# Backward weights loaded by transposing DMAs instead of TensorE transposes and a trip through DRAM

## The chip, the core and the metric

The kernel runs on one core of a Trainium2 chip. The metric is the device time of one execution in microseconds (us); three runs of the kernel before gave 1393.33, 1394.78 and 1395.50, median 1394.78. A core has five engines that run their own instruction streams: TensorE (PE; weight loads are shown as PEld), VectorE (DVE), ScalarE (ACT), GpSimd (POOL) and SyncE (SP). In this kernel SP issues nearly all DMAs; ScalarE issues those of the last stage.

## The reference, cut to what matters

Four residual layers, A, B, A, B, on a sequence of 2048 tokens of width 512 in bf16, with the same weights in both A layers and in both B layers. The outputs are the forward result and the gradients of the input and of five weight matrices.

```python
def _A_ref(x, wqkv, wo):            # wqkv (512, 1536), wo (512, 512), 32 heads of 16
    qkv = ...                        # x @ wqkv, split in q, k, v
    phi = lambda t: jnp.where(t > 0, t + 1, jnp.exp(t)) + 1e-6
    pq, pk = phi(q), phi(k)
    kv = jnp.einsum("bhsd,bhse->bhde", pk, v)
    z = jnp.einsum("bhsd->bhd", pk)
    ...
    o = num / den
    return o... @ wo
def _B_ref(x, w_gate, w_up, w_down): # (512, 1376), (512, 1376), (1376, 512)
    h = _sigmoid(x @ w_gate) * (x @ w_up)
    return h @ w_down
x = x + _A_ref(_layernorm(x), A_wqkv, A_wo)
x = x + _B_ref(_layernorm(x), B_w_gate, B_w_up, B_w_down)
x = x + _A_ref(_layernorm(x), A_wqkv, A_wo)
x = x + _B_ref(_layernorm(x), B_w_gate, B_w_up, B_w_down)
# and jax.vjp of all this against grad_out
```

Forward, a weight is used as it lies in DRAM. Backward, the gradient with respect to a layer's input needs each weight transposed: wdT, wuT, wgT for a B layer, woT and wqkvT for an A layer.

## The kernel before, in words

The sequence is cut into 16 tiles of 128 tokens (index `st`). The residual stream stays in SBUF as 16 tiles `x`. The stages follow each other as the program text has them; a scheduler then fixes the order of each engine's instructions ahead of the run, and may move instructions of a later stage into gaps of an earlier one. Each engine runs its list in order. A DMA waits in its queue for its data, for its destination to be free, and for the eighth DMA before it (eight semaphores are used in turn).

Start: `load_stream` (L95-109) loads x in four batches, with wqkv in between; x is cast to f32 on VectorE and ScalarE, `layernorm_tile` makes the normalised tile `hstage` (L310, ScalarE), and TensorE transposes it (`ln_tp`, L318).

Forward A layer, `a_fwd`. First half, for each tile: 12 matmuls with wqkv (`mm_ps`, L468), the exponentials, pq and pk, and four transposes of pq (`tp`, L318 by a helper). Then the small products kv and z. Second half, for each tile: `num_ps`, `den_ps`, the division (`ostage`), four transposes (`tp`), four matmuls with wo into `y_ps` (L542), a copy by ScalarE (L545) and the addition to x by GpSimd (L546).

Into the first half of both A layers, from tile 4 on, the caller puts a list of extra work, `extra`: the groups of `wT_groups` (L346-402), 26 of them in layer 0 and 24 in layer 2. A group transposes up to four blocks of 128x128 of a weight that lies in SBUF for the forward pass (TensorE, L372 for wg, wu, wqkv and wo; L396 for wd), into one PSUM tile `wt_ps`, which has one buffer; VectorE (L353) or ScalarE (L355) in turn copies it to a stage in SBUF, and SP stores the stage to DRAM (L377, L383, L400). The extra PSUM pool takes one of eight banks, so `mm_ps` has five buffers instead of six and `y_ps` one instead of two in these layers.

Forward B layer, `b_fwd`: gate and up products, sigmoid, transposes of the hidden tile, product with wd.

Backward: `b_bwd_p1(3)`, `a_bwd_p1(2)`, `b_bwd_p2(3)`, `b_bwd_p1(1)`, `a_bwd_p2(2)`, `a_bwd_p1(0)`, `b_bwd_p2(1)`, `a_bwd_p2(0)`. The p1 stages go through the tiles and make input gradients; the p2 stages make weight gradients with long sums over all tokens, and the scheduler moves their matmuls into the p1 stages where it can.

Each p1 stage starts with its weights. `load_b_weights` (L213-221) loads wdT, wuT and wgT, `load_a_weights` (L223-227) woT and wqkvT, all from the DRAM copies that the forward stages stored, on SP's queue. The pool for them has three places with one buffer each: w_a (wuT or wqkvT), w_b (wgT or woT) and w_c (wdT). So a load waits until the last use of what lay there. The first load of wdT waits for the end of the forward pass, as its SBUF was in use until then. In `b_bwd_p1`, `dhh_ps` (L760) uses wdT and `dh_ps` (L742) uses wuT and then wgT; in `a_bwd_p1`, `do_ps` (L958) uses woT and `dh_ps` (L1038) wqkvT. The loads `ssd_ld` (L751), `o_ld` and `pq_ld` (L696) and `p_set` (L811) go through the same queue.

Of the kernel before, what the change touches and what calls it, by code (L numbers as in the profile page):

```python
# [8 lines left out]
BF16 = mybir.dt.bfloat16  # L9
# [8 lines left out]
D = 512  # L18
# [32 lines left out]
def kernel(  # L51
# [70 lines left out]
    for l in range(4):  # L122
# [11 lines left out]
    k.wT = dict(  # L134
        wqkvT=dram.tile([3 * D, D], BF16, name="wqkvT_d"),
        woT=dram.tile([D, D], BF16, name="woT_d"),
        wgT=dram.tile([F, D], BF16, name="wgT_d"),
        wuT=dram.tile([F, D], BF16, name="wuT_d"),
        wdT=dram.tile([D, F], BF16, name="wdT_d"),
    )  # L140
# [11 lines left out]
    with tc.tile_pool(name="wfwd", bufs=1) as wfwd:  # L152
# [17 lines left out]
        with ExitStack() as lctx:  # L170
# [7 lines left out]
            if phases != "fwd":  # L178
                wtg = wT_groups(k)
                half = 26  # L180
                with tc.tile_pool(name="wt_stage", bufs=2) as wt_stage:
                    a_fwd(k, 0, lns[0], nxt=lns[1],
                          extra=lambda ps_pool: [g(wt_stage, ps_pool) for g in wtg[:half]])
                b_fwd(k, 1, lns[1], nxt=lns[2])
                with tc.tile_pool(name="wt_stage2", bufs=2) as wt_stage:
                    a_fwd(k, 2, lns[2], nxt=lns[3],
                          extra=lambda ps_pool: [g(wt_stage, ps_pool) for g in wtg[half:]])
            else:
                a_fwd(k, 0, lns[0], nxt=lns[1])
                b_fwd(k, 1, lns[1], nxt=lns[2])  # L190
                a_fwd(k, 2, lns[2], nxt=lns[3])
# [17 lines left out]
    with ExitStack() as bctx:  # L209
# [3 lines left out]
        def load_b_weights():  # L213
            k.wdT = wb.tile([P, NDC, F], BF16, name="wdT", tag="w_c")
            nc.sync.dma_start(out=k.wdT[:], in_=k.wT["wdT"].rearrange("(c p) f -> p c f", p=P))
# [130 lines left out]
def wT_groups(k):  # L346
    nc = k.nc
    groups = []
    cnt = [0]

    def evac(dst, src):
        if cnt[0] % 2 == 0:
            nc.vector.tensor_copy(dst, src)  # L353
        else:
            nc.scalar.copy(dst, src)  # L355
        cnt[0] += 1

    for w_sb, wT_d, C in ((k.wg, k.wT["wgT"], F), (k.wu, k.wT["wuT"], F),
                          (k.wqkv, k.wT["wqkvT"], 3 * D), (k.wo, k.wT["woT"], D)):
        ncc = (C + P - 1) // P  # L360
        for cc0 in range(0, ncc, 4):
            ccs = list(range(cc0, min(cc0 + 4, ncc)))
            holder = {}
            for j, cc in enumerate(ccs):
                def g(stage, ps_pool, w_sb=w_sb, wT_d=wT_d, C=C, cc0=cc0, ccs=ccs, j=j, cc=cc, holder=holder):
                    if j == 0:
                        holder["t"] = stage.tile([P, 4, D], BF16, name="wt_st")
                    st_t = holder["t"]
                    r = min(P, C - cc * P)
                    ps = ps_pool.tile([P, NDC, P], BF16, name="wt_ps")  # L370
                    for rc in range(NDC):
                        nc.tensor.transpose(ps[0:r, rc, :], w_sb[:, rc, cc * P:cc * P + r], k.ident[:])  # L372
                    evac(st_t[0:r, j, :], ps[0:r, :, :].rearrange("p a b -> p (a b)"))
                    if j == len(ccs) - 1:
                        nfull = len([c_ for c_ in ccs if min(P, C - c_ * P) == P])
                        if nfull > 0:
                            nc.sync.dma_start(  # L377
                                out=wT_d[cc0 * P:(cc0 + nfull) * P, :].rearrange("(n p) d -> p n d", p=P),
                                in_=st_t[:, 0:nfull, :])
                        if nfull < len(ccs):  # L380
                            c_ = ccs[nfull]
                            r_ = C - c_ * P
                            nc.sync.dma_start(out=wT_d[c_ * P:c_ * P + r_, :], in_=st_t[0:r_, nfull, :])  # L383
                groups.append(g)
    for cc in range(NDC):
        holder = {}
        for fs in range(3):
# [722 lines left out]
```

## Time and profile before

| what | value |
|---|---|
| median of three runs | 1394.78 us (1393.33 to 1395.50) |
| profiled execution, span from the first to the last instruction | 1393.1 us; the page has no other time of it |
| DMA traffic | 269.77 MB, mean 194 GB/s |
| transposes of `wt_ps` (L372, L396) | 196, each 218 ns long, between 34.0 and 290.6 us |
| copies of `wt_ps` (L353, L355) | 25 of about 0.42 us on VectorE, 25 of about 0.58 us on ScalarE |
| issue of wdT, wqkvT, woT, and issue to landing | 482.8 and 633.4 us, 6.6 to 6.9; 640.3 and 1025.8, 7.4 to 7.6; 642.7 and 1028.2, 6.5 to 6.7 |
| wuT and wgT main parts | 484.7 and 788.6 us; 488.9 and 701.7 us; 7.1 to 10.1 us to landing |
| first use of wdT, wuT, wgT, woT, wqkvT | 489.5, 498.0, 501.6, 650.2, 707.0 us |

The profile comes from one profiled execution. "Busy" of TensorE counts each matmul's whole way through the array, and matmuls overlap, so the distance from one start to the next tells more of the cost than a duration does. An arrow `<-` after an idle time names what ended the wait. "SPq" is SP's queue; the time beside a DMA there is its issue, not its transfer.

### The profile page before, as it was taken

How to read it: one execution, taken by the hardware profiler on the slowest of the kernel's cores; microseconds unless marked ns; L12 is line 12 of the kernel's file. 1: busy time of each engine (PE TensorE's matmuls, PEld its weight loads, DVE VectorE, ACT ScalarE, POOL GpSimd, SP SyncE). 2: the span in 40 equal slices, each digit the busy share in tenths (PEclk: the TensorE clock that was granted, in tenths of full speed). 3: DMA queues.
4: the chain of work that ended last, by engine and by line, in shares of the span. 5: the costliest groups of instructions: out<-in, count | busy, mean ns of one | idle time of the engine just before them, and what ended most of it. 6: DMA issues, size and time to landing. Idle time of an engine off the chain costs nothing. (4 is left out here: it accounts for less than half of the span.)

```text
span 1393.1 us, 25045 instructions
## 1 busy us (share of the span) xinstructions
PE 1297.9 (93%) x9956; PEld 790.1 (57%) x9956; DVE 679.9 (49%) x1468; ACT 647.3 (46%) x1168; POOL 250.5 (18%) x413
## 2 busy tenths in 40 slices
PE   4989899998899898998999999999999999988988
PEld 2555455556455444554665677555548675556767
DVE  6664644567533355665857400456640676611111
ACT  5857576775776544443547411444431447600000
POOL 4026654105633300002100100010010101100000
PEclk9999999999999999999999999999999999999999
DMA  7622334452543497547774586964568956499745
GB/s 273 230 103 103 149 152 158 147 177 98 201 178 143 169 326 259 175 168 237 218 230 148 181 227 149 334 217 167 172 199 248 275 169 192 143 311 261 175 122 162
DMA packets 268853, 269.77 MB, mean 194 GB/s; under 512 B 24576, under 2 KB 245184, under 8 KB 268736
## 3 DMA queue, kind: packets, MB, share of 16 engines
q1 hardware_dynamic: 246272, 253.50, 57.2%
q10 hardware_dynamic: 22464, 14.68, 3.6%
q8 instruction: 78, 1.28, 0.4%
q14 instruction: 39, 0.32, 0.1%
HBM read 144.57 MB, written 123.57 MB: 192 GB/s over the span
## 5 line engine op out<-in xcount | busy, mean ns | idle before, releaser
L730 ACT COPY ddT<-T_ps 128x1024 bf16<-128x1024 bf16 (+1 forms) x96 | 83.1, 867 | 103.4 <-PE T_ps L728 103.3
L630 POOL TENSOR_TENSOR ssd_t<-hh_t,oms 128x512 bf16<-128x512 bf16 (+1 forms) x96 | 100.6, 1052 | 83.0 <-ACT oms L628 48.4
L648 DVE SCALAR_TENSOR_TENSOR junk<-t_sb,h_ld 128x512 bf16<-128x512 f32 x64 | 46.1, 720 | 137.6 <-ACT t_sb L646 136.6
L762 DVE TENSOR_TENSOR dd_t<-dhh_ps,ssd_ld 128x512 bf16<-128x512 f32 (+1 forms) x96 | 60.4, 629 | 102.0 <-PE dhh_ps L760 102.0
L742 PEld LDWEIGHTS <-ddT 128*128 128x128 bf16 (+1 forms) x704 | 66.3, 98 | 71.4 <-issue 12.5
L468 PE MATMUL mm_ps<-wqkv,hT 128*128 128x512 bf16 x384 | 100.2, 386 | 0.5 <-DVE x_108 L601 0.4
L742 PE MATMUL dh_ps<-wuT,ddT 128*128 128x512 bf16 (+1 forms) x352 | 96.5, 382 | 3.9 <-ACT t_sb L646 0.9
L833 PE MATMUL p_ps<-p_set,p_a_15354 128*128 128x256 bf16 (+1 forms) x768 | 82.5, 267 | 10.8 <-DVE dw_stg L798 10.8
L629 DVE TENSOR_TENSOR hh_t<-u_ps,ssd_t 128x512 bf16<-128x512 f32 (+1 forms) x96 | 60.7, 634 | 65.3 <-PE u_ps L624 50.3
L760 PE MATMUL dhh_ps<-wdT,gT 128*128 128x512 bf16 (+1 forms) x384 | 87.8, 364 | 5.0 <-DMA wdT<-wdT_d 4.3
L624 PE MATMUL u_ps<-wu,hT 128*128 128x512 bf16 (+1 forms) x384 | 92.4, 361 | 0.0
L621 PE MATMUL g_ps<-wg,hT 128*128 128x512 bf16 (+1 forms) x384 | 92.0, 361 | 0.4 <-DVE ostage L530 0.4
L833 PE MATMUL p_ps<-p_set,p_a_10151 128*128 128x256 bf16 (+1 forms) x768 | 81.5, 261 | 0.9 <-DMA p_set<-sv_hdd_130 0.9
L599 PE MATMUL y_ps<-wd,hhT 128*128 128x512 bf16 (+1 forms) x352 | 81.4, 380 | 0.0
L742 PE MATMUL dh_ps<-wgT,ddT 128*128 128x512 bf16 (+1 forms) x352 | 81.3, 379 | 0.0
L833 PEld LDWEIGHTS <-p_a_15354 128*128 128x128 bf16 x768 | 68.9, 100 | 21.7 <-issue 8.4
L590 ACT COPY hhT<-hhT_ps 128x512 bf16<-128x512 bf16 (+1 forms) x96 | 49.5, 515 | 58.3 <-PE hhT_ps L587 58.1
L728 PEld LDWEIGHTS <-dd_t 128*128 128x128 bf16 (+1 forms) x704 | 50.7, 101 | 40.8 <-DVE dd_t L762 18.5
L833 PEld LDWEIGHTS <-p_a_10151 128*128 128x128 bf16 x768 | 67.2, 98 | 9.2
L728 PE MATMUL T_ps<-ident,dd_t 128*128 128x128 bf16 (+1 forms) x704 | 66.4, 221 | 3.6 <-DVE dd_t L762 3.5
L838 DVE TENSOR_TENSOR dw_stg<-p_ps,dw_stg 128x512 bf16<-128x512 f32 (+1 forms) x36 | 23.4, 653 | 87.5 <-PE p_ps L833 74.4
L1038 PE MATMUL dh_ps<-wqkvT,dkvT 128*128 128x512 bf16 x256 | 65.6, 380 | 0.0
(493 smaller groups left out, 2498.3 us busy)
## 6 DMA issues: line engine op xcount, KB each, us to landing
p_set<-sv_hdd_130 SPq DMA_DIRECT2D x15, 1024.0 KB, 7.1
p_set<-sv_hdd_119 SPq DMA_DIRECT2D x15, 1024.0 KB, 6.3
sv_ssd_118<-ssd_t SPq DMA_DIRECT2D x16, 688.0 KB, 3.1
sv_ssd_129<-ssd_t SPq DMA_DIRECT2D x16, 688.0 KB, 3.1
ssd_ld<-sv_ssd_129 SPq DMA_DIRECT2D x16, 688.0 KB, 5.5
sv_hdd_130<-dd_t SPq DMA_DIRECT2D x16, 688.0 KB, 3.9
ssd_ld<-sv_ssd_118 SPq DMA_DIRECT2D x16, 688.0 KB, 6.0
sv_hdd_119<-dd_t SPq DMA_DIRECT2D x16, 688.0 KB, 3.7
```

The source lines that it names most:

```text
L468: nc.tensor.matmul(ps[:], lhsT=hT[:, kc, :], rhs=k.wqkv[:, kc, n * D:(n + 1) * D], start=(kc == 0), stop=(kc == NDC - 1))
L599: nc.tensor.matmul(y_ps[:], lhsT=T["hhT"][0:r, fc, :], rhs=k.wd[0:r, fc, :], start=(fc == 0), stop=(fc == NFC - 1))
L621: nc.tensor.matmul(g_ps[:, 0:w], lhsT=hT[:, kc, :], rhs=k.wg[:, kc, c0:c0 + w], start=(kc == 0), stop=(kc == NDC - 1))
L624: nc.tensor.matmul(u_ps[:, 0:w], lhsT=hT[:, kc, :], rhs=k.wu[:, kc, c0:c0 + w], start=(kc == 0), stop=(kc == NDC - 1))
L629: nc.vector.tensor_tensor(hh_t[:, c0:c0 + w], u_ps[:, 0:w], ssd_t[:, 0, c0:c0 + w], ALU.mult)
L630: nc.gpsimd.tensor_tensor(ssd_t[:, 1, c0:c0 + w], hh_t[:, c0:c0 + w], oms[:, 0:w], ALU.mult)
L728: nc.tensor.transpose(tps[0:r, a, i, :], dd[:, a, fc * P:fc * P + r], k.ident[:])
L730: nc.scalar.copy(ddT[:, :, fcs[0]:fcs[0] + nfull, :], tps[:, :, 0:nfull, :])
L742: nc.tensor.matmul(dh_ps[:], lhsT=T["ddT"][0:r, a, fc, :], rhs=wT[0:r, fc, :], start=(i == 0), stop=(i == n_mm - 1))
L760: nc.tensor.matmul(dhh_ps[:, 0:w], lhsT=gT[:, jc, :], rhs=k.wdT[:, jc, c0:c0 + w], start=(jc == 0), stop=(jc == NDC - 1))
L833: nc.tensor.matmul(psv[:, icl, :], lhsT=lhs_all[:, st, ic * P:(ic + 1) * P], rhs=set_t[:, st, 0:W], start=(st == 0), stop=(st == NST - 1))
L1038: nc.tensor.matmul(dh_ps[:], lhsT=lhsT, rhs=k.wqkvT[:, n * NDC + c, :], start=(i == 0), stop=(i == 3 * NDC - 1))
```

## The change

The DRAM copies of the transposed weights, `wT_groups`, and the `extra` argument of `a_fwd` go. The two loaders read the weights themselves from the inputs, with a DMA that transposes. wu and wg have 1376 = 10 x 128 + 96 columns; their last 96 columns are first copied to a small DRAM tensor of 128 columns (`wtail`, filled up with the first 32 columns), by four DMAs that stand at the start of the program, and are transposed from there. The two PSUM pools get back the bank that `extra` took.

```diff
-    k.wT = dict(
-        wqkvT=dram.tile([3 * D, D], BF16, name="wqkvT_d"),
...
+    k.wtail = {nm: dram.tile([D, P], BF16, name=f"wtail_{nm}") for nm in ("wg", "wu")}
+    for nm, w_in in (("wg", B_w_gate), ("wu", B_w_up)):
+        nc.sync.dma_start(out=k.wtail[nm][:, 0:FLAST], in_=w_in[:, F - FLAST:F])
+        nc.sync.dma_start(out=k.wtail[nm][:, FLAST:P], in_=w_in[:, 0:P - FLAST])
...
-                wtg = wT_groups(k)
-                half = 26
-                with tc.tile_pool(name="wt_stage", bufs=2) as wt_stage:
-                    a_fwd(k, 0, lns[0], nxt=lns[1],
-                          extra=lambda ps_pool: [g(wt_stage, ps_pool) for g in wtg[:half]])
...
+            a_fwd(k, 0, lns[0], nxt=lns[1])
+            b_fwd(k, 1, lns[1], nxt=lns[2])
+            a_fwd(k, 2, lns[2], nxt=lns[3])
...
         def load_b_weights():
             k.wdT = wb.tile([P, NDC, F], BF16, name="wdT", tag="w_c")
-            nc.sync.dma_start(out=k.wdT[:], in_=k.wT["wdT"].rearrange("(c p) f -> p c f", p=P))
+            nc.sync.dma_start_transpose(out=k.wdT[:], in_=B_w_down[:, :])
             k.wuT = wb.tile([P, NFC, D], BF16, name="wuT", tag="w_a")
             k.wgT = wb.tile([P, NFC, D], BF16, name="wgT", tag="w_b")
-            for t_sb, t_d in ((k.wuT, k.wT["wuT"]), (k.wgT, k.wT["wgT"])):
-                nc.sync.dma_start(out=t_sb[:, 0:NFC - 1, :],
-                                  in_=t_d[0:(NFC - 1) * P, :].rearrange("(c p) j -> p c j", p=P))
-                nc.sync.dma_start(out=t_sb[0:FLAST, NFC - 1, :], in_=t_d[(NFC - 1) * P:F, :])
+            for t_sb, w_in, nm in ((k.wuT, B_w_up, "wu"), (k.wgT, B_w_gate, "wg")):
+                nc.sync.dma_start_transpose(out=t_sb[:, 0:NFC - 1, :], in_=w_in[:, 0:(NFC - 1) * P])
+                nc.sync.dma_start_transpose(out=t_sb[:, NFC - 1, :], in_=k.wtail[nm][:, :])
 
         def load_a_weights():
             k.woT = wb.tile([P, NDC, D], BF16, name="woT", tag="w_b")
-            nc.sync.dma_start(out=k.woT[:], in_=k.wT["woT"].rearrange("(c p) j -> p c j", p=P))
+            nc.sync.dma_start_transpose(out=k.woT[:], in_=A_wo[:, :])
             k.wqkvT = wb.tile([P, 3 * NDC, D], BF16, name="wqkvT", tag="w_a")
-            nc.sync.dma_start(out=k.wqkvT[:], in_=k.wT["wqkvT"].rearrange("(c p) j -> p c j", p=P))
+            nc.sync.dma_start_transpose(out=k.wqkvT[:], in_=A_wqkv[:, :])
...
-def wT_groups(k):
...
-def a_fwd(k, l, ln, nxt=None, extra=None):
+def a_fwd(k, l, ln, nxt=None):
...
-        if extra is not None:
-            ps_extra = ctx.enter_context(tc.tile_pool(name=f"af_ps_extra{l}", bufs=1, space=PSUM))
...
-                tc.tile_pool(name=f"af_ps_mm{l}", bufs=(5 if extra is not None else 6), space=PSUM) as ps_mm:
+                tc.tile_pool(name=f"af_ps_mm{l}", bufs=6, space=PSUM) as ps_mm:
...
-                if extra is not None and st == 4:
-                    extra(ps_extra)
...
-                tc.tile_pool(name=f"af_ps_y{l}", bufs=(1 if extra is not None else 2), space=PSUM) as ps_y:
+                tc.tile_pool(name=f"af_ps_y{l}", bufs=2, space=PSUM) as ps_y:
```

In the built program the transposing DMAs stand in SP's queue at the places that the plain loads had, up to one or two neighbours. TensorE's list loses the 196 transposes; its order in the backward stages stays nearly the same.

More of the change, by code (lines that the diff above doesn't have):

```diff
@@ L133 @@
         k.sv[l] = d
-    k.wT = dict(
-        wqkvT=dram.tile([3 * D, D], BF16, name="wqkvT_d"),
[L136 to L140, printed above, removed]
+    k.wtail = {nm: dram.tile([D, P], BF16, name=f"wtail_{nm}") for nm in ("wg", "wu")}
+    for nm, w_in in (("wg", B_w_gate), ("wu", B_w_up)):
+        nc.sync.dma_start(out=k.wtail[nm][:, 0:FLAST], in_=w_in[:, F - FLAST:F])
+        nc.sync.dma_start(out=k.wtail[nm][:, FLAST:P], in_=w_in[:, 0:P - FLAST])
     k.dwp = dict(
@@ L177 @@
             lns = [FwdLN(k, l) for l in range(4)]
-            if phases != "fwd":
-                wtg = wT_groups(k)
-                half = 26
-                with tc.tile_pool(name="wt_stage", bufs=2) as wt_stage:
-                    a_fwd(k, 0, lns[0], nxt=lns[1],
-                          extra=lambda ps_pool: [g(wt_stage, ps_pool) for g in wtg[:half]])
[L184 to L191, printed above, removed]
+            a_fwd(k, 0, lns[0], nxt=lns[1])
+            b_fwd(k, 1, lns[1], nxt=lns[2])
+            a_fwd(k, 2, lns[2], nxt=lns[3])
             ostg = lctx.enter_context(tc.tile_pool(name="out0_stg", bufs=2))
@@ L343, in dram_batch @@
     return ap2d[batch_rows(b, nb), :].rearrange("(n p) d -> p n d", p=P)
-def wT_groups(k):
[L347 to L387, printed above, removed]
-            def g(stage, ps_pool, cc=cc, fs=fs, holder=holder):
-                if fs == 0:
-                    holder["t"] = stage.tile([P, F], BF16, name="wdt_st")
-                st_t = holder["t"]
-                fcs = fchunks_of_slice(fs)
-                ps = ps_pool.tile([P, NDC, P], BF16, name="wt_ps")
-                for i, fc in enumerate(fcs):
-                    r = fc_rows(fc)
-                    nc.tensor.transpose(ps[:, i, 0:r], k.wd[0:r, fc, cc * P:(cc + 1) * P], k.ident[0:r, 0:r])
-                c0, w = FSL[fs]
-                evac(st_t[:, c0:c0 + w], ps[:].rearrange("p a b -> p (a b)")[:, 0:w])
-                if fs == 2:
-                    nc.sync.dma_start(out=k.wT["wdT"][cc * P:(cc + 1) * P, :], in_=st_t[:])
-            groups.append(g)
-    return groups
```

## Prediction

> **What bounds the kernel now.** I read the page first, for the busiest engine, then the windows by stage, then TensorE's timeline at the places that the edit touches. The page's first group of lines says who sets the pace:
>
> ```profile
> PE 1297.9 (93%) x9956; PEld 790.1 (57%) x9956; DVE 679.9 (49%) x1468; ACT 647.3 (46%) x1168; POOL 250.5 (18%) x413
> ```
>
> TensorE is busy 93% of the span, so an instruction taken from its stream is time, and a wait put into it is time. The windows show where it still waits (columns: stretch, length, busy time and count of PE, PEld, DVE, ACT, POOL; granted clock; DMA share; GB/s):
>
> ```profile
> 19.67:81.00 61.33, 59.53 (x424) 31.31 (x423) 40.76 (x91) 50.10 (x90) 4.19 (x11) 1.00 0.60 206
> 482.80:498.00 15.20, 9.47 (x59) 5.17 (x56) 5.22 (x9) 5.08 (x8) 0.00 (x0) 0.78 0.98 315
> 640.00:660.00 20.00, 15.49 (x108) 7.84 (x106) 10.46 (x25) 6.47 (x12) 7.49 (x13) 1.00 0.92 290
> 1025.00:1050.00 25.00, 21.73 (x141) 12.42 (x140) 8.89 (x20) 4.88 (x9) 5.13 (x9) 1.00 0.89 275
> ```
>
> The first row is the first half of a forward attention layer: TensorE is full, VectorE and ScalarE are not. The other three are the places where backward weights are loaded and soon used: the DMA engines are 89 to 98% busy there and TensorE has gaps. The timeline at the sharpest of them:
>
> ```profile
> 482.83 0.37 SPq L215 DMA_DIRECT2D wdT<-wdT_d  x1
> 484.76 0.38 PE L318 MATMUL gT_ps<-ident,gstage 128*128 128x128 bf16 x4 [0.67 <-ACT gT L327]
> 489.47 3.57 PE L760 MATMUL dhh_ps<-wdT,gT 128*128 128x512 bf16 x8 [4.33 <-DMA wdT<-wdT_d]
> 501.63 2.54 PE L742 MATMUL dh_ps<-wgT,ddT 128*128 128x512 bf16 x11
> ```
>
> wdT is issued at 482.83, lands 6.6 us later, and TensorE stands still for it. So any slower load of wdT costs its whole excess.
>
> **What goes: the transposes in the forward layers.** 196 transposes (L372 152, L396 44) leave TensorE, 25 copies of 0.42 us leave VectorE (L353), 25 of 0.58 us leave ScalarE (L355), and 16 stores leave SP's queue. A busy time of 218 ns per transpose would mislead, since matmuls overlap; the pace shows the cost:
>
> ```profile
> 67.85 0.40 PE L318 MATMUL tp<-ident,pqstage 128*128 128x128 bf16 x4
> 70.99 0.40 PE L318 MATMUL tp<-ident,pqstage 128*128 128x128 bf16 x4
> ...
> 264.75 0.40 PE L318 MATMUL tp<-ident,pqstage 128*128 128x128 bf16 x4
> ...
> 295.86 0.40 PE L318 MATMUL tp<-ident,pqstage 128*128 128x128 bf16 x4
> ```
>
> These `tp` transposes come once per tile of 128 tokens. Where no weights are transposed the step is 70.99-67.85 = 3.14 us. In layer 0 the nine steps from 32.02 to 67.85 take 35.83 us, 7.6 over nine steps of 3.14. In layer 2 the eight steps from 264.75 to 295.86 take 31.11, 6.0 over. The two pieces at 251.23 and 253.89 add 0.6 with their 0.40 idle. Sum: -14.2 us. A check from below: 50 groups at the 0.22 us from the start of one group to the next matmul make 11; the rest is waiting for `wt_ps`, which has one buffer. VectorE and ScalarE only get freer (ScalarE 50.1 of 61.3 us now), so nothing becomes late in their place. Bounds -11 and -15.
>
> **What comes back with the PSUM bank.** y_ps gets two buffers instead of one in both attention layers. Its matmuls start at 106.70, 108.45, 110.20, 111.96: 1.75 us apart, which is four matmuls (0.86), ScalarE's copy (0.58) and the handing over. TensorE's own work per tile is 0.86 + 0.22 (tp) + 0.22 (num) + 0.11 (den) = 1.41; GpSimd's addition takes 1.27. From 88.19 to 119.83 I count 25.4 us of such work in 31.6, so 6.2 of gaps, of which the first tiles and two waits for `hstage` stay. I take half: -3 per layer, -6. Bounds 0 and -10 (0.34 us for 15 tiles, twice). mm_ps gains a sixth buffer where no wait for it is seen: 0.
>
> **What is added at the start.** Four small DMAs (`wtail`) are queued on SP ahead of the first x load. SP's issues of its first loads take 0.39 to 0.48 us each, so x and wqkv move by 1.6 us. Their 2048 packets of 192 and 64 bytes have a near row, the `p_set` load of 96 columns (2048 packets of 192 bytes, 4.0 us to landing) against 2.2 us for the first 128 KB load: 1.8 us more. TensorE's first instruction, at 17.86, waits for `hstage`, which stands behind ScalarE's casts of the last x batch, and those stand behind the same DMA engines. I take +3, bounds 1.6 and 6 (both sides of a DRAM-to-DRAM copy slow).
>
> **What replaces the plain loads.** No transposing DMA is in this trace. The program as built moves blocks of 16 source rows by 128 columns: 256-byte reads, and 32 bytes to each of 128 partitions. Lower bound, it costs what the plain load costs: 6.6 us for wdT, nothing added. By packets, 192 bytes cost 1.8 us for 128 per engine, 14 ns each, and 512 bytes (`p_set`, 1024 KB, 6.3 us) 4.1 us, 32 ns; a line through both gives 17.6 ns for 256 bytes. wdT has 1376 x 4 = 5504 such rows, 344 per engine: 6.1 us, plus 2.2, 8.3 to landing. Upper bound, the 32-byte pieces cost a packet each: 44032/16 x 14 ns = 38.5 us, 40.7 to landing. I take 17.6 ns, since the 192- and 512-byte rows enclose 256 bytes, and nothing in the trace prices the crossbar. With p us for a row on an engine:
> - wdT: 344p + 2.2 against 6.7: 344p - 4.5 = +1.6.
> - wgT, third in the queue behind wdT, out_0 (1.4) and wuT: lands at 482.8 + 2.2 + 1.4 + 1048p, used at 501.63 plus the shift before: 704p - 10.7 = +1.7.
> - woT at 640, behind wqkvT (384 + 128 rows): 640.28 + 2.2 + 512p against 650.23: +1.3.
> - woT at 1025: 1025.83 + 2.2 + 512p = 1037.0, used after 1038.7: 0; the 46 matmuls of L885 hide it.
> - wdT (633), wgT (701) and wuT (788) of layer 1 come over 80 us ahead of their use: 0 themselves. But o_ld, pq_ld, ssd_ld stand behind transposes on SP's queue, and each DMA waits for the eighth before it: +1.5, bounds 0 and 5.
>
> Sum +6.1.
>
> The measured row that a rule bears on is this plain wdT load, 1.41 MB in 6.6 us. The Trainium skill, "DMA: Bandwidth & Descriptors", section "Latency and other measured facts", gives DMA transposes 261 GB/s effective; wdT would then move in about 5.4 us (estimate) and the whole sum would be about 6 us lower than mine. Against the change speaks "VectorE: DVE Perf Modes", section "The three transpose paths": 1309 ns for one 128x128 block on the crossbar against 390 on TensorE; 43 blocks one after another would be 56 us (estimate), hundreds of us in all. TensorE's own transposes cost 55 ns of pace here, and no row decides between the two figures.
>
> **Sum.** The span is 1393.1 us, 1.7 below the median of the runs, 1394.78; I add the difference back. 1394.8 - 14.2 - 6 + 3 + 6.1 = 1383.7, say 1384.
>
> **Rivals.**
> 1. Slower: the transposing load is the new wait. Its terms above sum to 2072p - 33.7 once all are positive. Against a gain of 17.2 - 1.5 it decides from p = 24 ns, where wdT lands after 10.5 us instead of 6.7. At 35 ns: +39 + 1.5 - 17.2 = +23, 1418; at 50 ns: +70 + 1.5 - 17.2 = +54, 1449; at the 32-byte bound (112 ns) +198 and more, near 1580, and then layer 1's loads block the queue too. For it: 98% DMA share at 482.8 and no slack for wdT. Against it: bytes and queue are the same as before.
> 2. About the same: the forward gain is half given back, because the next wait in the forward layers (ScalarE's `hstage`, VectorE's pq_t, GpSimd's 1.27) is right behind, and y_ps gives nothing. -7 + 3 + 3 gives about 1393. Against it: the steps of 3.14 us stand in the same layers with all of these engines at work.
> 3. Faster than the forecast: transposes as fast as plain loads and y_ps worth 5 per layer: -14.2 - 10 + 2 + 0 = 1373.
>
> **Chances.** Forecast 0.45, rival 3 0.08, rival 1 0.38 (0.01 of it within 0.2%), rival 2 0.09 (0.05 within 0.2%, 0.03 faster, 0.01 slower). What this kernel's runs can tell from no change is about 0.2%, 3 us. Faster 0.45 + 0.08 + 0.03 = 0.56, same 0.06, slower 0.38. Rival 1 is spread, a little more than half of it below 1440. So 1374 to 1440 leaves out about 0.03 below and 0.17 above; the forecast's own range is 1376 to 1391.
>
> **What would show it.** Right: no L372/L396, `tp` steps of 3.14 us throughout, y_ps starts about 1.5 us apart, wdT landing in 8 to 9 us with TensorE's wait before dhh_ps near 6 us, and no new wait above 2 us at 650 and 1039. Wrong: wdT landing above 10.5 us; DMA waits before dh_ps (wuT, wgT) or do_ps (woT); SP's queue issuing a transpose for several us and o_ld or ssd_ld late behind it; a first TensorE instruction later than 24 us.

## The result, and the profile after

The changed kernel takes 1409.29 us (median of four runs, 1404.11 to 1412.63), the kernel before 1395.14 beside it (1393.33 to 1397.55). The ratio is 1.0101, with a 95% interval of 1.0077 to 1.0123: slower by about 14 us, where the forecast was 11 us faster. The profiled execution has a span of 1408.3 us and a time of 1410.03.

The first group of lines of the page, and the windows at the four places that were shown of before (columns: stretch, length, busy time and count of PE, PEld, DVE, ACT, POOL; granted clock; DMA share; GB/s):

```profile
PE 1287.9 (91%) x9760; PEld 780.1 (55%) x9760; DVE 671.4 (48%) x1443; ACT 636.1 (45%) x1143; POOL 251.3 (18%) x413
```

```profile
23.40:76.80 53.40, 51.84 (x319) 24.72 (x318) 35.69 (x78) 43.30 (x77) 4.16 (x11) 1.00 0.50 171
484.61:501.38 16.77, 8.53 (x59) 4.62 (x56) 5.22 (x9) 4.81 (x8) 0.00 (x0) 0.69 1.09 215
642.00:665.85 23.85, 17.56 (x108) 9.18 (x106) 11.22 (x25) 6.66 (x12) 7.59 (x13) 0.86 0.97 252
1033.49:1061.97 28.48, 23.39 (x141) 13.34 (x140) 8.90 (x20) 4.89 (x9) 5.15 (x9) 0.94 0.87 244
```

TensorE has 10 us less to do and a span that is 15 us longer. The stretches run between the same matmuls as before, to 0.1 us: the first half of layer 0 went from 61.3 to 53.4 us, and the three places with weight loads from 15.2, 20.0 and 25.0 to 16.8, 23.9 and 28.5, with a lower granted clock in each.

The timeline where the first wdT is loaded, and the pace of the `tp` transposes in layer 0:

```profile
484.65 5.59 SPq L201 DMA_TRANSPOSE wdT<-in_B_w_down_dram  x1
486.57 0.38 PE L303 MATMUL gT_ps<-ident,gstage 128*128 128x128 bf16 x4 [0.67 <-ACT gT L312]
490.92 6.57 SPq L205 DMA_TRANSPOSE wuT<-in_B_w_up_dram  x1
493.79 3.57 PE L682 MATMUL dhh_ps<-wdT,gT 128*128 128x512 bf16 x8 [6.84 <-DMA wdT<-in_B_w_down_dram]
498.85 5.34 SPq L205 DMA_TRANSPOSE wgT<-in_B_w_gate_dram  x1
506.58 1.67 PE L664 MATMUL dh_ps<-wgT,ddT 128*128 128x512 bf16 x7 [1.41 <-DMA wgT<-in_B_w_gate_dram]
...
57.40 0.40 PE L303 MATMUL tp<-ident,pqstage 128*128 128x128 bf16 x4
60.54 0.40 PE L303 MATMUL tp<-ident,pqstage 128*128 128x128 bf16 x4
```

wdT lands 9.1 us after its issue (the second time 7.4), and the transposing issues of wdT, wuT and wgT hold SP's queue for 5.3 to 6.6 us, where the plain one of wdT took 0.37 in the kernel before. The step of `tp` is 3.14 us, as predicted.

To see where time comes and goes, each matmul of a run is set beside the same one of the kernel before (the n-th of the same tile), and the difference of their starts is listed. This is worked out from the traces; a rise from one row to the next is time lost between them:

| place (start in the kernel before, us) | after | e1 | e2 | e5 | e3 |
|---|---|---|---|---|---|
| first matmul (17.9) | +3.7 | 0.0 | +3.0 | +3.9 | +4.0 |
| layer 0, end of the first half (80.9) | -4.2 | 0.0 | -4.6 | -4.1 | -4.2 |
| layer 1, behind its first tile (127.7) | 0.0 | +4.3 | -1.2 | -4.3 | -0.3 |
| layer 2, end of the first half (312.0) | -6.1 | +4.3 | -7.2 | -10.4 | -6.4 |
| layer 3, behind its first tile (365.4) | +2.3 | +9.9 | -1.6 | -10.6 | +1.8 |
| end of the forward pass (480.2) | +1.8 | +9.4 | -2.1 | -10.6 | +1.4 |
| first dhh_ps (489.5) | +4.3 | +9.5 | -1.2 | -9.6 | +1.5 |
| a_bwd_p1 of layer 2 under way (661.6) | +5.8 | +6.6 | +1.9 | -8.3 | -1.3 |
| a_bwd_p1 of layer 0 under way (1051.0) | +12.0 | +9.2 | +6.4 | +1.4 | -1.0 |
| last p_ps (1388.9) | +14.7 | +9.0 | +8.4 | +2.4 | +1.4 |

(e1 to e5 are experiments below.) In the column "after" the first halves give 7.9 and 6.1 us, but between the end of the first half and the next layer 4.1 and 8.3 us go again, so the forward pass ends 1.8 us late; the backward pass then loses 12.9. Each column is a single trace, and the places where the clock falls differ from trace to trace: e16 below, whose forward pass is that of the changed kernel, loses 5.2 us in place of 8.3 at the second passage. A rise in one column is good to some 3 us; what the medians of runs say goes before it.

The waits of TensorE name the new ones (columns: who waits for whom; us in total, times, longest). After:

```profile
PE dhh_ps L682 <- DMA wdT<-in_B_w_down_dram: 6.8, 1, 6.8
PE tp L303 <- DVE ostage L452: 4.6, 7, 0.9
...
PE p_ps L755 <- DMA p_a<-sv_h: 3.4, 1, 3.4
...
PE g_ps L543 <- DVE zfull L489: 3.1, 2, 2.2
PE y_ps L464 <- ACT oT L312: 2.8, 6, 1.0
PE den_ps L446 <- DVE dtmp L449: 2.6, 5, 1.4
...
PE do_ps L880 <- DMA woT<-in_A_wo_dram: 1.4, 1, 1.4
```

Before:

```profile
PE y_ps L542 <- ACT y_sb L545: 1.7, 4, 0.5
...
PE tp L318 <- DVE ostage L530: 0.9, 2, 0.4
...
PE den_ps L524 <- DVE dtmp L527: 0.4, 2, 0.2
```

The waits for ostage, dtmp and oT lie in the second halves of the A layers, where y_ps's number of buffers was changed; the wait for zfull lies at the passage to the B layer and did not exist before. The wait that a second buffer takes away, that of y_ps for ScalarE's copy y_sb, was 1.7 us in all.

TensorE's list shows what else is different at the passage: where the first g_ps of layer 1 stands, before and after.

```profile
114.80 0.59 PE L621 MATMUL g_ps<-wg,hT 128*128 128x512 bf16 x2
```

```profile
118.47 1.04 PE L543 MATMUL g_ps<-wg,hT 128*128 128x512 bf16 x4 [0.89 <-DVE zfull L489]
```

Before, g_ps and u_ps matmuls of the B layer stand between the last groups of y_ps, from 114.80 on; the last group starts at 118.97. So the gaps that one y_ps buffer leaves there were already filled. After, all of g_ps stands behind the last y_ps (116.09) and waits for zfull.

### The profile page after: what moved, and what is told of

Same layout as the page of the kernel before. It is cut to its first block, busy times and chain, and to the rows that moved or that the text cites. A ratio compares the mean times of both kernels' runs of the same rounds, so it can differ in the third digit from the quotient of the medians.

```text
span 1408.3 us, 24551 instructions
## 1 busy us (share of the span) xinstructions
PE 1287.9 (91%) x9760; PEld 780.1 (55%) x9760; DVE 671.4 (48%) x1443; ACT 636.1 (45%) x1143; POOL 251.3 (18%) x413
## 5 line engine op out<-in xcount | busy, mean ns | idle before, releaser
L755 PE MATMUL p_ps<-p_set,p_a 128*128 128x256 bf16 (+1 forms) x1920 | 207.4, 266 | 15.9 <-DVE dw_stg L720 9.6
L755 PEld LDWEIGHTS <-p_a 128*128 128x128 bf16 x1920 | 174.0, 99 | 40.5 <-issue 10.3
L390 PE MATMUL mm_ps<-wqkv,hT 128*128 128x512 bf16 x384 | 94.0, 384 | 0.6 <-DVE x L523 0.6
L785 PE MATMUL p_ps<-p_a,p_set 128*128 128x512 bf16 (+1 forms) x352 | 83.7, 379 | 3.3 <-DVE dw_stg L760 3.3
L572 POOL TENSOR_SCALAR ab<-c 128x2 f32<-128x2 f32 x64 | 12.3, 192 | 413.3 <-DVE junk L570 413.3
L568 ACT ACTIVATE t_sb<-dh_ps,rstd_all 128x512 f32<-128x512 f32 x64 | 44.0, 687 | 85.0 <-PE dh_ps L664 54.0
L598 POOL TENSOR_SCALAR gstage<-x 128x512 bf16<-128x512 f32 x48 | 33.2, 713 | 242.8 <-PE gT_ps L303 178.7
```

The lines of the kernel that those rows point to most:

```text
L390: nc.tensor.matmul(ps[:], lhsT=hT[:, kc, :], rhs=k.wqkv[:, kc, n * D:(n + 1) * D], start=(kc == 0), stop=(kc == NDC - 1))
L755: nc.tensor.matmul(psv[:, icl, :], lhsT=lhs_all[:, st, ic * P:(ic + 1) * P], rhs=set_t[:, st, 0:W], start=(st == 0), stop=(st == NST - 1))
L785: nc.tensor.matmul(ps[0:r, :], lhsT=st_t[:, st, j * P:j * P + r], rhs=g_all[:, st, :], start=(st == 0), stop=(st == NST - 1))
```

## The experiments

Two questions: what undoes the gain of the forward pass, and what the transposing loads cost. Each run was timed in five rounds beside the kernel before on the same chip (its medians there: 1393.97 for e1 to e4, 1394.1 for e5 to e8, 1395.36, 1396.34, 1393.99 and 1394.11 for e12, e14, e15 and e16, 1395.01 for e17 and e18; e13 was timed with e12). Ratios are to those runs.

**e1: the second y_ps buffer alone, in the kernel before.**

```diff
+            ps_extra = ectx.enter_context(...)   # closed after the first half
-                tc.tile_pool(name=f"af_ps_y{l}", bufs=(1 if extra is not None else 2), space=PSUM) as ps_y:
+                tc.tile_pool(name=f"af_ps_y{l}", bufs=2, space=PSUM) as ps_y:
```

> The kernel before, with one part of the change alone: the bank of wt_ps is given back after the first half of the A layer, and y_ps gets two buffers; the TensorE transposes and the plain loads stay. Theory A (the second y_ps buffer costs time: it reorders the second half of the A layer and the passage to the B layer, where after the change TensorE arrives 4.1 us later in layers 0-1 and about 7 us later in layers 2-3, measured from the end of the first half): about 1395 + 11 = 1406 us, u_ps of layer 3 starting some 6 us later than before, g_ps waiting for zfull. Theory B (what was lost in the forward pass comes from the absence of the transposes or from the clock, and y_ps is worth what the prediction said): 1389 to 1395 us.

Measured: 1402.37 us, ratio 1.0055 (1.0041 to 1.0069), 8 us slower. TensorE's waits in this run:

```profile
PE tp L318 <- DVE ostage L532: 4.5, 7, 0.9
...
PE g_ps L623 <- DVE zfull L569: 3.1, 2, 2.2
...
PE den_ps L526 <- DVE dtmp L529: 2.6, 5, 1.4
```

They are those of the changed kernel to a tenth of a us, without any transposing load. The buffer that was to bring 6 us costs time: its column rises by 4.3 and 5.6 at the same places. Theory B falls.

**e2: the changed kernel with one y_ps buffer.**

```diff
-                tc.tile_pool(name=f"af_ps_y{l}", bufs=2, space=PSUM) as ps_y:
+                tc.tile_pool(name=f"af_ps_y{l}", bufs=1, space=PSUM) as ps_y:
```

> The changed kernel with one buffer for y_ps, nothing else altered. Theory A: the second halves and passages go at about their old pace, 1409 - 11 = 1398 us, and TensorE's first dhh_ps comes at about 483 us instead of 493.8. Theory B: 1409 us or, if two buffers are worth 3 us per layer, up to 1415.

Measured: 1403.97 us, ratio 1.0079 (1.0060 to 1.0099): 3 us less than the changed kernel by the ratios, whose intervals overlap, where theory A asked for 11. The waits tell what is missing:

```profile
PE g_ps L543 <- DVE zfull L489: 4.9, 2, 4.2
...
PE tp L303 <- DVE ostage L452: 0.9, 2, 0.4
```

The second half is as before (ostage 0.9), the passage is not: g_ps waits for zfull even longer. So the number of buffers explains the second half, and something else the passage. In the order in which the pools are opened, the kernel before has eight banks as: ln_tp, wt_ps, tp, four of num_ps and den_ps, y_ps; the B layer opens ln_tp, two hhT_ps, four of g_ps and u_ps, y_ps, so its g_ps and u_ps come to lie on num_ps and den_ps. Without the bank of wt_ps all moves down by one, and one of these four banks is that of y_ps, which zfull's product uses last. This is theory D.

**e5: the same with a bank held.**

```diff
+        ps_res = ctx.enter_context(tc.tile_pool(name=f"af_ps_res{l}", bufs=1, space=PSUM))
+        res_ps = ps_res.tile([P, NDC, P], BF16, name="res_ps")
+        nc.tensor.transpose(res_ps[:, 0, :], k.ident[:], k.ident[:])
...
-                tc.tile_pool(name=f"af_ps_mm{l}", bufs=6, space=PSUM) as ps_mm:
+                tc.tile_pool(name=f"af_ps_mm{l}", bufs=5, space=PSUM) as ps_mm:
```

> The changed kernel with one buffer for y_ps, five for mm_ps, and one PSUM bank held by a small tile through both halves of the A layer, as wt_ps held it before (one transpose and one copy more per layer, 0.4 us). Theory D (the time lost at the passage from the A to the B layer comes from the placing of the banks: without the held bank the first g_ps and u_ps of the B layer fall on the bank of y_ps and on TensorE's list behind zfull, and the layer-norm chain is put ahead of hh_t): the passages go as before, TensorE reaches the backward pass at 480.2 - 10.2 us, and the time is 1409 - 12 = 1397 us. Theory E (the passages are slow because the transposes are gone, whatever the banks): as with one buffer alone, 1404 us.

Measured: 1397.58 us, ratio 1.0021 (1.0008 to 1.0034), as theory D said (the places of the banks are read from the order of the pools; no trace shows a bank). TensorE's waits:

```profile
PE tp L303 <- DVE ostage L457: 0.9, 2, 0.4
...
PE g_ps L548 <- DVE ostage L457: 0.4, 1, 0.4
```

No wait for zfull is left, and the column of e5 keeps the whole gain of the first halves up to 480 us. In e5 the first g_ps stands between the y_ps groups again, as in the kernel before (at 110.54, the last y_ps group at 114.71); in e2 it comes at 117.31, behind all of them. An idle PSUM bank is worth 6 to 8 us here (6 by the medians, 8 by the ratios, 1.0079 against 1.0021), by where it puts the banks of the next layer and with them the order of TensorE's list. The five buffers of mm_ps are no part of it: up to 80.9 us the columns of e2 and e5 agree to 0.5 us.

**e13: two y_ps buffers without the collision.** Plain loads and late wtail as in e6 below; the pools of the second half are opened in the order tp, y_ps, num and den, those of the B layer in the order y_ps, hhT_ps, g_ps and u_ps.

```diff
-                tc.tile_pool(name=f"af_ps_nd{l}", bufs=2, space=PSUM) as ps_nd, \
-                tc.tile_pool(name=f"af_ps_y{l}", bufs=2, space=PSUM) as ps_y:
+                tc.tile_pool(name=f"af_ps_y{l}", bufs=2, space=PSUM) as ps_y, \
+                tc.tile_pool(name=f"af_ps_nd{l}", bufs=2, space=PSUM) as ps_nd:
...
```

> As the run with all three suspects taken out (plain loads of other data, so the transposed weights are wrong; wtail late), but with two buffers for y_ps, and the PSUM pools opened in another order, so that g_ps and u_ps of the B layer lie on the banks of num_ps and den_ps and not on those of y_ps. If two buffers hurt by the collision of banks alone, and are worth the 3 us per layer of the prediction: 1382 - 6 = 1376 us. If the second half is slower by itself with two buffers (1.4 us per layer in the run of the kernel before with two buffers): 1384 to 1386 us; and if the passage is slow too, 1390 us or more.

Measured: 1386.77 us, ratio 0.9944 (0.9925 to 0.9963), against 0.9913 (0.9897 to 0.9928) of e6. The wait for zfull is gone, those of the second half are not:

```profile
PE tp L304 <- DVE ostage L453: 4.4, 7, 0.8
```

So two buffers are not worth 3 us per layer in either of the two places tried; the run is about 4 us slower than e6. With them TensorE's list runs ahead of the division (ostage) and stops there. Why the scheduler then orders it so was not tried.

**e3: plain loads in place of the transposing ones.**

```diff
-            nc.sync.dma_start_transpose(out=k.wdT[:], in_=B_w_down[:, :])
+            nc.sync.dma_start(out=k.wdT[:], in_=B_w_gate.rearrange("(c p) f -> p c f", p=P))
...
```

> The changed kernel with every transposing load replaced by a plain load of the same size and shape out of another input (wdT from B_w_gate, wuT and wgT from B_w_down, woT from A_wo, wqkvT from x), so the weights are wrong and the loads cost what they cost before. Theory A: the transposing loads cost what the offset between the traces gains from 482 us on, 14.7 - 1.8 = 12.9 us, 1409 - 13 = 1396 us; dhh_ps waits 4.3 us for wdT as before. Theory B (the loads cost the 6.1 us of the prediction and the rest of the backward offset has other reasons): about 1403 us. Rival C (all of the loss is the loads'): 1381 us or less.

Measured: 1396.00 us, ratio 1.0017 (1.0004 to 1.0030). Against 1.0101 that is 0.84%, some 12 us for the transposing loads, twice the 6.1 of the prediction; the column of e3 is level from 480 us on, to within 3 us. Theory A fits, rival C (all of the loss) falls.

**e8: wdT alone transposed.**

```diff
 # as e3, but
+            nc.sync.dma_start_transpose(out=k.wdT[:], in_=B_w_down[:, :])
```

> As the run with plain loads of other data, but wdT alone is loaded by the transposing DMA (the other transposed weights are wrong). If each transposing load costs its later landing alone: 1396 + 2.5 = 1399 us, with the wait before dhh_ps at 6.8 us. If the first load sets off the rest (half-speed stretches, the queue): 1402 us or more.

Measured: 1398.46 us, ratio 1.0029 (1.0015 to 1.0042), 2.5 us over e3 by the medians, as the first theory said, and 1.7 by the ratios. The intervals overlap, and the two profiled executions have the same span (1395.6 us), so the difference is not shown. What the traces show is the place: TensorE's wait for wdT in e3 and in e8 is

```profile
PE dhh_ps L683 <- DMA wdT<-in_B_w_gate_dram: 4.4, 1, 4.4
```

```profile
PE dhh_ps L683 <- DMA wdT<-in_B_w_down_dram: 5.3, 1, 5.3
```

0.9 us longer, and not at the 6.8 us of the expectation. A stretch at half clock lies over the wait and behind it, 10.2 us long in e8 and 6.8 in e3; TensorE works for 5.6 and 3.1 us of it, so at most 1.3 us more are lost (half of the difference). What wuT, wgT, woT and wqkvT cost singly was not run.

**The half-speed stretches.** The windows of the changed kernel, laid on the places where the granted clock is low:

```profile
487.60:497.80 10.20, 4.01 (x15) 1.77 (x14) 1.69 (x3) 0.00 (x0) 0.00 (x0) 0.50 1.27 262
654.90:661.70 6.80, 4.95 (x29) 3.01 (x29) 4.75 (x11) 1.33 (x3) 2.44 (x4) 0.50 0.63 211
1054.20:1057.60 3.40, 3.40 (x20) 2.26 (x19) 0.00 (x0) 0.69 (x1) 0.00 (x0) 0.50 0.89 292
```

and of the kernel before and of e3 at the first of them:

```profile
488.60:495.40 6.80, 5.93 (x26) 3.11 (x26) 2.87 (x5) 1.25 (x2) 0.00 (x0) 0.50 1.09 357
```

```profile
487.20:494.00 6.80, 3.05 (x8) 1.13 (x8) 1.09 (x2) 0.00 (x0) 0.00 (x0) 0.50 1.04 347
```

The clock is either whole or 0.50, for 3.4 us or a multiple of it, and each of these three stands at or behind a wait of TensorE. From 480 to 1060 us the changed kernel has 20.4 us at half speed, e3 6.8. But time is lost there only while TensorE works: in the first stretch of the changed kernel it stands for wdT until 493.79 and works for 4.0 of the 10.2 us. Half of the work in the three stretches is (4.01 + 4.95 + 3.40) / 2 = 6.2 us, in e3's it is 3.05 / 2 = 1.5, so the half clock makes at most 4.7 us of the 12. The rest are waits. The Trainium skill, "TensorE: Matmul & The Clock Gate", section "Part 1: The HAM clock gate", says that TensorE's clock has two states, whole and half, set by activity in free-running windows of about 3.4 us; the traces agree with the two states and the length. The page lets a window without work bring the half state; here waits of 1.38, 0.73 and 1.29 us in a row, at 652 to 657, went ahead of the second stretch.

**e17: a late woT with plain loads.** Where TensorE's wait for woT stands, its issue stood 6.3 us behind that of wqkvT on SP's queue.

```diff
 # as e3, and
+            nc.sync.dma_start(out=k.woT[0:1, 0, 0:64], in_=k.wqkvT[0:1, 0, 0:64])   # lands before woT may be loaded
             nc.sync.dma_start(out=k.woT[:], in_=A_wo.rearrange("(c p) j -> p c j", p=P))
```

> As the run with plain loads of other data (the transposed weights are wrong), but the load of woT is made to wait for the landing of wqkvT (a copy of 128 bytes of wqkvT into woT stands between them), so that woT lands some 10 to 12 us after the issue of wqkvT, as in the changed kernel, where its issue stands behind the 6.2 us that wqkvT's transposing issue takes. Queue and transfers are plain otherwise. If the late woT is what the A weights cost (offsets of 3.7 us at 650 and 3.5 us at 1041 in the changed kernel, half-speed stretches among them): 1396 + 7 = 1403 us. If do_ps has slack for it: 1396 to 1398 us.

Measured: 1401.15 us, ratio 1.0043 (1.0029 to 1.0058), 4 to 5 us over e3. woT's load was issued 9.8 us behind wqkvT's, later than meant, so TensorE waited longer than in the changed kernel (6.3 us at 653, 2.7 at 1044), and a stretch at half speed came with it:

```profile
PE do_ps L882 <- DMA woT<-in_A_wo_dram: 9.0, 2, 6.3
```

```profile
650.00:660.20 10.20, 6.17 (x26) 3.21 (x26) 3.38 (x7) 1.76 (x3) 1.20 (x2) 0.50 1.08 299
```

do_ps has no slack for a late woT at either place. The size is not the one of the changed kernel, whose own wait is 1.4 us.

**e16: SP's queue held, loads plain.**

```diff
 # as e3, and behind each of wdT, wuT, wgT, wqkvT
+            nc.sync.dma_start(out=k.hold[0:1, :], in_=k.wdT[0:1, 0, 0:64])   # waits for the landing
```

> As the run with plain loads of other data (the transposed weights are wrong), and behind each of wdT, wuT, wgT and wqkvT a store of 128 bytes of the loaded tile to a DRAM scratch, queued on SP. It waits for the load's landing, so SP's queue is held for some 6 to 7 us after each load, as a transposing issue holds it for 5.4 to 6.6, while the loads themselves are plain and land early. Theory Q (the queue: ssd_ld, o_ld, pq_ld, pk_ld, stores and the next weight behind the held queue come late): 1396 + 6 to 12 = 1402 to 1408 us. Theory L (the later landing of the weights themselves, with the half-speed stretches behind those waits): 1396 to 1399 us.

Measured: 1392.97 us, ratio 0.9997 (0.9987 to 1.0007): not more than e3 (the intervals overlap). The timeline of SP's queue shows that it was held:

```profile
487.49 0.29 SPq L203 DMA_DIRECT2D hold<-wdT  x1
...
488.21 0.42 SPq L207 DMA_DIRECT2D wgT<-in_B_w_down_dram  x1
492.75 0.23 SPq L210 DMA_DIRECT2D hold<-wuT  x1
```

The first store waits until 487.49 for wdT, the second until 492.75 for wuT, and wgT goes out at 488.21 between them; no matmul is late for it. So theory Q falls for the holds that this run made. At the first B layer they were shorter than meant, 4.1 to 4.3 us each: wgT went out 7.3 us behind wdT, against 6.5 in e3 and 14.2 in the changed kernel, and woT went out ahead of its hold. The run does not clear the queue of the changed kernel. There woT stands behind wqkvT's issue (first three lines; the last two are of e3):

```profile
642.27 6.20 SPq L212 DMA_TRANSPOSE wqkvT<-in_A_wqkv_dram  x1
648.56 1.67 SPq L210 DMA_TRANSPOSE woT<-in_A_wo_dram  x1
...
653.35 1.02 PE L880 MATMUL do_ps<-woT,gT 128*128 128x512 bf16 x4 [1.38 <-DMA woT<-in_A_wo_dram]
```

```profile
638.96 0.38 SPq L213 DMA_DIRECT2D wqkvT<-in_A_x_dram  x1
641.34 0.38 SPq L211 DMA_DIRECT2D woT<-in_A_wo_dram  x1
```

woT went out 6.3 us behind wqkvT instead of 2.4, and landed 4.8 us after its own issue, sooner than a plain load of it (6.5 to 6.7). It was late by the queue, not by its transfer. The first wgT can be read the same way: it landed 7.7 us after its issue, where the plain one of the kernel before took 10.0.

**e15: the plain loads cut in pieces.** wdT in 12 plain DMAs, the others in 4 to 12.

```diff
+            for c in range(NDC):
+                for p0, p1 in ((0, 43), (43, 86), (86, P)):
+                    nc.sync.dma_start(out=k.wdT[p0:p1, c, :], in_=B_w_gate[c * P + p0:c * P + p1, :])
```

> As the run with plain loads of other data (the transposed weights are wrong), but each load is cut into 4 to 12 plain DMAs, so that SP's queue is held about as long as by a transposing one (12 issues of 0.4 to 0.5 us, against 5.4 to 6.6 us for one transposing issue), while the bytes and the layout of the transfer stay plain. Theory Q (the time on SP's queue is what makes the transposing loads dear, by late landings and by what is queued behind them): 1396 + 8 to 12 = 1404 to 1408 us, dhh_ps first 2 to 3 us later than with whole plain loads. Theory L (it is the transfer itself, beyond the issue): 1396 to 1399 us.

Measured: 1449.40 us, ratio 1.0394 (1.0372 to 1.0415), far beyond both theories. The pieces did not go out at 0.4 us each:

```profile
484.71 29.84 SPq L203 DMA_DIRECT2D wdT<-in_B_w_gate_dram  x10
```

Ten pieces of 42 or 43 partitions took 29.8 us on the queue (the ten of wgT, with 128 partitions each, 5.8), so the run imitated nothing of the changed kernel and decides nothing between Q and L. Each piece also waits for the eighth DMA before it, so issue and landing are not told apart here. What it shows by itself: wdT cut into pieces of partitions like this is no way to load it early.

**e4: wtail later.**

```diff
-    for nm, w_in in (("wg", B_w_gate), ("wu", B_w_up)):     # ahead of the first x load
...
+        for nm, w_in in (("wg", B_w_gate), ("wu", B_w_up)): # behind the load of wd
```

> The changed kernel with the four wtail DMAs queued behind the load of wd instead of ahead of the first x load. If the four DMAs at the head delay the whole start, as TensorE's first instruction at 21.58 instead of 17.86 us says: that instruction at about 17.9 us and 1409 - 3.7 = 1405.5 us. If the start is made up later (the first stages wait for something else): 1409 us.

Measured: 1407.48 us, ratio 1.0093 (1.0078 to 1.0109), hardly below 1.0101. The first matmul is back at 17.70, and the forward pass ends 4.5 us earlier than in the changed kernel (-2.7 in place of +1.8); the end is at +14.4 all the same. Within the span its trace has 58.0 us at half speed against 47.8, so at most 5.1 us more are lost there, which would be about the difference. Why there are more such stretches is open.

**e6: all three suspects out.** Plain loads (e3), one y_ps buffer with the bank held (e5), late wtail (e4).

> All three suspects taken out together: plain loads of other data of the same size in place of the transposing ones (so the transposed weights are wrong), wtail behind the load of wd, one y_ps buffer with the bank held. If the three are the whole loss, what is left is the gain of 14 us from the first halves: 1394 - 14 = 1380 us. If something else costs time, above 1385.

Measured: 1382.28 us, ratio 0.9913 (0.9897 to 0.9928), 2 us over the expectation. The gain of the first halves is there, and the three suspects hold nearly all of the loss. It bounds what a load that costs no more than a plain one could bring.

**e7: a version meant to beat both.** Late wtail, the bank held, wdT and woT loaded once, by transposing DMAs, in the forward pass into places of their own.

```diff
+            k.wdT = keep.tile([P, NDC, F], BF16, name="wdT")      # ahead of b_fwd(1)
+            nc.sync.dma_start_transpose(out=k.wdT[:], in_=B_w_down[:, :])
+            k.woT = keep.tile([P, NDC, D], BF16, name="woT")
+            nc.sync.dma_start_transpose(out=k.woT[:], in_=A_wo[:, :])
```

> A version meant to beat both kernels: transposing loads kept, wtail behind the load of wd, one y_ps buffer with the bank held, and wdT and woT loaded once in the forward pass into places of their own (wdT was loaded twice and woT twice). If waiting for wdT and woT is most of what the transposing loads cost, TensorE's waits of 6.8 us for wdT and 1.4 us for woT and the half-speed stretches behind them go, and some 3 us of SP's queue held by wuT, wgT and wqkvT stay: 1380 - 7 + 3 = 1376 to 1385 us. If the cost lies in SP's queue wherever the loads stand: 1390 us or more.

Measured: 1396.37 us, ratio 1.0020 (1.0007 to 1.0034): a miss. The waits for wdT and woT are gone, and this one is new:

```profile
PE gT_ps L303 <- DMA h_ld<-sv_h: 17.9, 1, 17.9
```

gstage and h_ld of the first backward tile stand behind the transposing issues of wuT and wgT, 5.1 and 5.6 us, on SP's queue, and go out at 483, when TensorE has stood since 468. Here, too, the held queue costs, as what stands behind it is needed at once. A version with those two loads ahead of the weights was not run.

**e12 and e14: the kernel before, weights loaded in the shadow of layer 3.** The pool of the backward weights is opened on the other side of SBUF before b_fwd(3), with its loads; in e14 the stages gstage, h_ld and ssd_ld of the B layers' backward pass lie there too.

```diff
+            wb = ctx.enter_context(tc.tile_pool(name="wbwd", bufs=1, side="right"))
+            load_b_weights()                                       # ahead of b_fwd(3)
 # e14 also, three pools of b_bwd_p1:
+        stg = ctx.enter_context(tc.tile_pool(name=f"bb_stg{l}", bufs=2, side="right"))
```

> The kernel before, transposes on TensorE and plain loads kept, but the pool of the backward weights is opened before the last forward layer (on the other side of SBUF, where a B layer leaves room), so that wdT, wuT and wgT are loaded while that layer runs. If the exposed place of the first wdT load is what makes any load there dear (TensorE's wait of 4.3 us before dhh_ps and the half-speed stretch behind it, 3.4 us): 1394 - 7 = 1387 us. If the loads disturb the stores of the last forward layer, or the next wait (gstage) comes in their place: 1391 to 1394 us.

Measured: 1402.36 us, ratio 1.0061 (1.0038 to 1.0084). The wait for wdT is gone, and in its place stands

```profile
PE gT_ps L318 <- DMA gstage<-in_grad_out_dram: 9.6, 1, 9.6
```

since gstage had come to lie elsewhere in SBUF and went out at 490.3 only; e14, which moves it again, has no such wait.

> As the run of the kernel before with early weight loads, but the stages of the first backward layer (gstage, h_ld, ssd_ld) also lie on the other side of SBUF. In that run gstage had come to lie where out_t of the last forward layer lay, was issued at 490.3 us, and TensorE waited 9.6 us for it, more than the 4.3 us for wdT that had gone. If that place was the whole miss, the wait goes and dhh_ps starts some 5 us earlier than in the kernel before: 1394 - 4.3 - 1.7 to 3.4 (half-speed stretches) = 1386 to 1388 us. If the time at the start of the backward pass is taken by something next (ssd_ld, the copy of gT): 1391 us or more.

Measured: 1395.17 us, ratio 0.9995 (0.9984 to 1.0007). dhh_ps starts 3.6 us earlier than in the kernel before, but layer 3 pays 2.2 us for the loads that run beside its stores, T_ps then waits up to 2.4 us for dd_t, and the rest is gone by the end. The place where the first wdT load is exposed cannot simply be emptied.

**e18: the stores of e16 in the kernel before.**

> The kernel before with the same 128-byte stores behind wdT, wuT, wgT and wqkvT as in the run that held SP's queue, which took 3 us less than plain loads without them. If lining up the weight loads one behind the other helps by itself: 1394 - 3 = 1391 us. If that difference came from something else in that pair of runs: 1394 us.

Measured: 1392.89 us, ratio 0.9984 (0.9971 to 0.9998). This version is below both kernels, by 2 us against the one before, about as much as these runs can tell from nothing. That the order of the loads is the reason is argued, not shown.

## Why the prediction was wrong

- **The transposes' -14.2** was right: -7.9 and -6.1, 14.0 us, with steps of 3.14 us. The pace, not the busy time, was the right price.
- **y_ps, -6, is the step that failed.** With the bank it was worth about +11 us (0.8% between the changed kernel and e5). In the trace that is 1.4 in each second half, 2.8 and 5.5 at the passages, 0.3 back; another 1.3 went between the halves of layer 2, in a half-speed stretch of 6.8 us in place of 3.4, which e16's trace does not have. Taking the gaps of 6.2 us in 31.6 as something that a buffer would fill was wrong twice. The list of waits had only 1.7 us in which y_ps waited for ScalarE's copy, and the B layer's g_ps and u_ps already stood in the last of the gaps. With two buffers TensorE waits for ostage, dtmp and oT instead (e1, e13), and g_ps comes behind zfull. The bounds 0 and -10 left out a loss, though the edit changes the scheduler's order and the place of the PSUM banks opened behind it. The sentence "mm_ps gains a sixth buffer where no wait for it is seen: 0" was right for mm_ps and blind to the bank (e2 against e5: 6 to 8 us).
- **The start, +3**, measured +3.7, as first seen by TensorE; e4 shows it in the forward pass, and not in the end.
- **The transposing loads, +6.1**, measured about 12: the second term that failed, by its size. Its price of a row was right: the changed kernel's trace holds wdT as 5504 packets of 256 bytes, 18 ns each (median), against 17.6 forecast. The landings were near the forecast: wdT 9.1 us and 7.4 against 8.3, TensorE's wait 6.8 against near 6, wgT's wait 1.4 (forecast 1.7), woT's 1.4 (1.3). What was too small is the rest. The columns "after" and e3 differ by 2.8 us at the first dhh_ps, by 7.1 at 661.6, 13.0 at 1051.0 and 13.3 at the end. In these stretches TensorE waits 1.0 us more than in e3 for dnA near 657, 0.8 more for pk_ld and v_ld near 720, 2.0 for dw_stg near 824 and 1.3 more for p_a near 1053, and at most 4.7 us go at half speed (e3 in turn waits 1.5 us for p_set near 641, which the changed kernel does not). The 1.5 us for the queue did not hold these waits, and the half clock had no term.
- **The two rules on transposes** that the prediction weighed, from the Trainium skill, "DMA: Bandwidth & Descriptors" (261 GB/s) and "VectorE: DVE Perf Modes" (1309 ns for a block): wdT's 1.41 MB in 7.4 to 9.1 us make 155 to 190 GB/s, and 172 to 212 ns for each of 43 blocks. These times run from issue to landing. By them the rate lies below the first rule, and the time of a block is a sixth to an eighth of the second.
- **Rival 1** came out on the right side for a reason that was not its own: wdT landed before its threshold of 10.5 us, and the loss that turned the sign lay in the forward pass. **Rival 2** (the forward gain half given back) was the nearest, by its outcome and not by its waits: the whole gain was given back, and to ostage, dtmp, oT and zfull.
- **What would show it wrong** named a queue that issues a transpose for several us, and that was seen. e16's shorter holds cost nothing, but woT and, in e7, gstage and h_ld were late behind such issues.

Sum by the trace: -14.0 + 10.8 + 1.3 + 3.7 forward, and +12.9 backward, are +14.7, the last row of the table.

## What to carry to other kernels

A freed PSUM bank is not free: it changes the place of the banks opened after it, across layers, and with it what the next layer's first matmuls wait for. So price an extra buffer with both signs, take its gain from the waits that the trace names, look whether the next stage's work already fills the gaps, and compare the built order at the next stage's start. A wait of TensorE can cost more than its length where the clock falls behind it; add half of TensorE's work in such a stretch, not half of the stretch, as part of it lies inside the wait.

A load that is moved out of an exposed place leaves the place to the next load in line (e7, e12): name what stands behind it, in the queue and in SBUF, first.

## What the hardware showed that had not been expected

- A transposing issue holds SP's queue for longer, the more blocks of 128x128 it moves. In the changed kernel it was 1.7 to 2.3 us for 16 (woT), 5.3 to 6.6 for 40 (wuT, wgT), 5.4 to 5.6 for 43 (wdT), 5.9 to 6.2 for 48 (wqkvT), so 0.10 to 0.16 us a block; the 4 blocks of a tail took 1.2 to 2.8. The plain issues of wdT, woT and wqkvT in the kernel before took 0.37 us each.
- The granted clock falls to 0.50 for 3.4 us or multiples of it, and each such piece costs up to 1.7 us, less where TensorE stands still in it: at most 23.9 us in the changed kernel's profile, 17.1 in the one before, over the whole span. The three shown above stand at or behind waits of TensorE. Another begins between 73 and 83 us, at or near the end of the one-column matmuls of z_ps, in every trace here but that of e12, with no wait of a few us ahead of it.
- wdT in pieces of 42 or 43 partitions goes out at 3 us a piece on one queue, the wait for the eighth DMA before included (e15).
